# Batch 0's attention in two-bank tiles, scores in another order, and batch 1's loads moved off ScalarE: one attention + MLP kernel on one Trainium2 core

## The chip, the cores and the metric

The kernel runs on one NeuronCore of a Trainium2 chip. The metric is the device time of one execution in microseconds (us); before the change the median of five runs is 300.94 us (300.72 to 301.49). The engines are named as in the profile: PE is TensorE (PEld its weight loads), DVE VectorE, ACT ScalarE, POOL GpSimd, SP SyncE. ACTq and SPq are the instruction queues of ACT and SP when they issue a DMA.

## The reference

The computation is attention with pooled keys and values, followed by an MLP over all tokens. There are 8 batches, 8 heads, 576 tokens a batch and a head size of 64.

```python
k_p = k.reshape(B, H, Sp, 8, D).mean(axis=3)          # 576 keys become 72
v_p = v.reshape(B, H, Sp, 8, D).mean(axis=3)
scores = scale * np.matmul(q, k_p.transpose(0, 1, 3, 2))
scores = scores - np.max(scores, axis=-1, keepdims=True)
attn = np.exp(scores)
attn = attn / (np.sum(attn, axis=-1, keepdims=True) + 1e-09)
attn_out = np.matmul(attn, v_p)                       # [8, 8, 576, 64]
x = attn_out.transpose(0, 2, 1, 3).reshape(4608, 512)
h = x @ w_in                                          # [4608, 2048]
out = (h - np.tanh(h)) @ w_out                        # [4608, 512]
```

## The kernel before

**Attention of one batch.** Two heads have 144 pooled keys together, and the kernel calls this a pair. The first 128 key rows of each of the four pairs are one tile each; the 16 left over of each pair share a fifth tile, the leftover tile (index `NM`), at 32 rows a pair. `pool_k` adds the eight raw rows of each key, `turn_tile` transposes the pooled keys on PE, and `kb_main` and `kb_left` place them in `KB`. The queries are cast to bf16 (`q_turn` for batch 0, `q_cast` for the others) and transposed on PE (`q_pe_transpose`, one pair of heads a call). `scores_wide` multiplies them for 512 of the 576 query columns and ACT takes the exponential into `E`; the last 64 columns come later through `q_pe_tail` and `scores_tail`, which are called the tail. `av_half` multiplies `E` by the pooled values `VB` for one block of 128 queries and one half of the heads: three matmuls, the third for the leftover keys. `VB` carries a column of constants, so the sum of the exponentials comes out beside each head. DVE then takes the reciprocal of the four sums (L359) and multiplies (L360). The result `x_sb` is transposed into `xT`, for batches 0 and 1 on PE with a copy by ACT (`x_pe_transpose`, L390 and L397).

**MLP.** Tokens are worked in nine groups of 512. For each group there are 16 hidden blocks of four matmuls (L428, one for each feature block of `xT`), ACT's tanh (L439) and DVE's subtraction (L441); then four blocks of output tokens with 16 matmuls each (L456). Group 0 needs batch 0's attention alone. Batch 1's attention is woven into group 0's output matmuls, four of them at a step u = 0 to 15, and later batches into the group before the one that needs them.

**Order.** The order of the work on each engine is written out by hand: the program runs in the order of the source (`manual_schedule`), each engine takes its instructions in that order, and semaphores are set where one engine needs another's result. A DMA that is issued by an engine stands in that engine's order, with its waits.

**The head.** Nothing dense can run until batch 0's queries, keys and values are loaded, pooled, scored and normalised, and `xT` is filled. `warm_pe` puts matmuls with no use of their own into that time (L527). Batch 0's q comes in three loads that ACT issues (L534), its leftovers of k and v in two more (L111), its q tail in another (L640, between the second and third exponential). Its v is loaded as bf16 by POOL and pooled by PE (`v_pe_pool`, L618). The opening halves of hidden blocks 0 to 4 (`mlp_h_mms(0, i, 0, 2)`) are run as soon as feature blocks 0 and 1 of `xT` are there.

**Loads.** SP issues k, q and v of batch 1 after batch 0's k. The load of k waits for the second chunk of `w1` (L592). POOL issues the four chunks of `w1` (L503) and of `w2` (L510): two of `w2` early, and two inside `pool_k` of batch 1, after its first addition. The leftover of batch 1's v is four loads of 16 rows, and its q tail one load; ACT issues these five (L106, L127) behind batch 0's exponentials.

**PSUM.** Three pools share the eight banks: `ps_h` with three, `ps_o` with two and `ps_a` with three. `ps_any` takes from `ps_a` and `ps_h` in turn, and from `ps_a` alone once the opening halves run.

Of the kernel before, what the change touches and what calls it, by code (L numbers as in the profile page):

```python
# [8 lines left out]
FP32 = mybir.dt.float32  # L9
BF16 = mybir.dt.bfloat16  # L10
# [9 lines left out]
R = 4  # L20
# [5 lines left out]
TG = 512  # L26
# [11 lines left out]
def kernel(  # L38
# [19 lines left out]
    ps_h = ctx.enter_context(tc.tile_pool(name="ps_h", bufs=3, space=PSUM))  # L58
    ps_o = ctx.enter_context(tc.tile_pool(name="ps_o", bufs=2, space=PSUM))
    ps_a = ctx.enter_context(tc.tile_pool(name="ps_a", bufs=3, space=PSUM))  # L60
# [14 lines left out]
    spread = const.tile([128, 128], BF16, name="spread")  # L75
    mask = const.tile([128, 3 * NM, 1], FP32, name="mask")
# [3 lines left out]
    q_bf = const.tile([128, R + 1, H, D], BF16, name="q_bf")  # L80
    warm = const.tile([128, 1], FP32, name="warm")
# [22 lines left out]
    def load_left(src, dst, b, eng=nc.sync):  # L104
        return [
            eng.dma_start(out=dst[32 * t : 32 * t + LO, NM, :], in_=src[b, 128:PR, t, :])  # L106
            for t in range(NM)
        ]
# [35 lines left out]
    def q_cast(b, eng=nc.gpsimd.tensor_copy, parts=1):  # L144
        t = q_raws.pop(b)
        n = H // parts
        for h in range(0, H, n):
            eng(  # L148
                out=q_bf[:, 0:R, h : h + n, :].rearrange("p j h d -> p h j d"),
                in_=t[:, h : h + n, 0:R, :],  # L150
            )
        eng(out=q_bf[:QT, R, :, :], in_=t[:QT, :, R, :])
# [61 lines left out]
    def pool_v(b, eng):  # L214
        r = v_raw[b % 2].rearrange("p t (j d) -> p t j d", d=D)
        eng.tensor_tensor(  # L216
            out=r[:, :, 0:4, :], in0=r[:, :, 0:4, :], in1=r[:, :, 4:8, :], op=ALU.add
        )
        eng.tensor_tensor(  # L219
            out=r[:, :, 0:2, :], in0=r[:, :, 0:2, :], in1=r[:, :, 2:4, :], op=ALU.add  # L220
        )
        eng.tensor_tensor(
            out=r[:, :, 0, :], in0=r[:, :, 0, :], in1=r[:, :, 1, :], op=ALU.add
        )
        v_main(VB[b % 2], r[:, :, 0:1, :], eng, 0, NM)
        v_left(VB[b % 2], r[:, NM, 0:1, :], eng)

    def v_main(vb, vs, eng, t0, t1):
        n = t1 - t0
        eng.tensor_tensor(  # L230
            out=vb[:, 2 * t0 : 2 * t1, 0:D].rearrange("p (t s) d -> p t s d", s=2),
            in0=vs[:, t0:t1, :, :].to_broadcast([128, n, 2, D]),
            in1=mask[:, 2 * t0 : 2 * t1, :]
            .rearrange("p (t s) o -> p t s o", s=2)
            .to_broadcast([128, n, 2, D]),
            op=ALU.mult,
        )

# [82 lines left out]
    def scores_wide(b, ts):  # L321
        if b not in E_tiles:
            E_tiles[b] = work.tile([128, NT, S], BF16, name="E", tag="E")
        E = E_tiles[b]
        for t in ts:
            ps = ps_any([128, QA], FP32, "s_ps")
            score_mms(b, t, ps[:, :], 0, QA)
            nc.scalar.activation(out=E[:, t, 0:QA], in_=ps[:, :], func=ACT.Exp, scale=SCALE)

# [8 lines left out]
    def av_half(b, blk, half, x_sb, alloc):  # L338
        E = E_tiles[b]
        vb = VB[b % 2]  # L340
        c0 = blk * 128 if blk < 4 else S - 128
        ps = alloc([128, 4, D1], FP32, "x_ps")
        for n in range(3):
# [14 lines left out]
        rden = work.tile([128, 4, 1], FP32, name="rden", tag="rden", bufs=4)  # L358
        nc.vector.reciprocal(out=rden[:, :, :], in_=ps[:, :, D:D1])  # L359
        nc.vector.tensor_tensor(  # L360
            out=x_sb[:, half, :, :],
            in0=ps[:, :, 0:D],
            in1=rden[:, :, :].to_broadcast([128, 4, D]),
            op=ALU.mult,
        )
# [56 lines left out]
    def mlp_h_mms(g, i, f0, f1, pool=None):  # L422
        tok0 = g * TG
        if f0 == 0:
            p, tag = pool or (ps_h, "hT_ps")
            h_tiles[i] = p.tile([128, TG], FP32, name="hT_ps", tag=tag)
        for fb in range(f0, f1):
            nc.tensor.matmul(  # L428
                h_tiles[i][:, :],
                lhsT=w1b[:, fb, i * 128 : (i + 1) * 128],  # L430
                rhs=xT[:, fb, tok0 : tok0 + TG],
                start=(fb == 0),
                stop=(fb == NFB - 1),
            )
# [88 lines left out]
    warm_ps = ps_o.tile([128, 512], FP32, name="warm_ps", tag="o_ps")  # L523
# [60 lines left out]
    load_w2(0)  # L584
    nc.gpsimd.tensor_copy(out=v_bf[:, NM, :], in_=v_raw[1][:, NM, :])
    load_w2(1)
# [5 lines left out]
    after(load_k(1), w1_dmas[1])  # L592
    load_q(1, False)
    load_main(v_pairs, v_raw[1], 1, 0, NM)

# [19 lines left out]
    def v_pe_pool(t0, t1, turn):  # L615
        ps = ps_any([128, t1 - t0, 1, D], FP32, "v_ps")
# [26 lines left out]
    pool_k(0, nc.vector, 2, 4)  # L643
    warm_pe(6)
    k_turn(2, 4)
    pool_k(0, nc.vector, NM, NT)
    warm_pe(2)
    q_pe_transpose(0, (2, 3), "act")
    warm_pe(2)
    scores_wide(0, (2, 3))  # L650
    k_turn_left()
    warm_pe(2)
    v_ps = v_pe_pool(NM, NT, spread)
    scores_wide(0, (NM,))
    v_left(VB[0], v_ps[:, 0, :, :], nc.vector)
    vs = v_pe_pool(0, NM, ident)
    v_main(VB[0], vs, nc.vector, 0, 2)
    v_main(VB[0], vs, nc.vector, 2, 4)
    load_left(v_pairs, v_raw[1], 1, nc.scalar)
    load_q_tail(1, q_raws[1], nc.scalar)  # L660
    xs = [new_x() for _ in range(4)]
    gts = []
    ps_o2 = lambda sh, dt, name: ps_o.tile(sh, dt, name=name, tag="o_ps")
    ps_h2 = lambda sh, dt, name: ps_h.tile(sh, dt, name=name, tag="hT_ps")
    warm_pe(2)
    av_half(0, 0, 0, xs[0], ps_all)
    av_half(0, 1, 0, xs[1], ps_all)
    av_half(0, 2, 0, xs[2], ps_all)
    x_pe_transpose(0, 0, xs[0], (0, 2))
    av_half(0, 3, 0, xs[3], ps_all)  # L670
    warm_pe(1)
    x_pe_transpose(0, 1, xs[1], (0, 2))
    ps_any = ps_b1
    av_half(0, 0, 1, xs[0], ps_h2)
    warm_pe(1)
    x_pe_transpose(0, 2, xs[2], (0, 2))
    av_half(0, 1, 1, xs[1], ps_b1)
    warm_pe(1)
    x_pe_transpose(0, 3, xs[3], (0, 2))
    av_half(0, 2, 1, xs[2], ps_o2)  # L680
    mlp_h_mms(0, 0, 0, 2)
    x_pe_transpose(0, 0, xs[0], (2, 4))
    av_half(0, 3, 1, xs[3], ps_b1)
    mlp_h_mms(0, 1, 0, 2)
    x_pe_transpose(0, 1, xs[1], (2, 4))
    mlp_h_mms(0, 2, 0, 2)
    x_pe_transpose(0, 2, xs[2], (2, 4))
    x_pe_transpose(0, 3, xs[3], (2, 4))
    mlp_h_mms(0, 3, 0, 2, (ps_o, "o_ps"))
    mlp_h_mms(0, 4, 0, 2, (ps_o, "o_ps"))  # L690
# [16 lines left out]
    pool_k(1, nc.gpsimd, mid=(2, 3))  # L707
# [5 lines left out]
    for u in range(16):  # L713
        qd, tb = u // 4, u % 4
        mlp_o(0, tb, qd * 4, qd * 4 + 4, gts, o_pools[tb])
        if u == 0:
            q_cast(1, nc.scalar.copy, 2)
# [4 lines left out]
        if u == 4:  # L722
            q_pe_transpose(1, (2,), "act")
            pool_v(1, nc.vector)
        if u == 5:
            q_pe_transpose(1, (3,), "act")
        if 4 <= u <= 8:
            scores_wide(1, (u - 4,))
        if u == 6:
            q_pe_tail(1)  # L730
        if u == 8:
            scores_tail(1)
# [72 lines left out]
```

The softmax here doesn't subtract the row's maximum and nothing guards it: scores larger than these inputs give would overflow.

## Time and profile before

| what | us |
|---|---|
| median of five runs | 300.94 |
| the profiled execution, its own time | 300.52 |
| its span in the profile | 298.8 |
| PE busy | 289.7 (97%) |
| DVE busy | 159.1 (53%) |
| ACT busy | 149.3 (50%) |
| POOL busy | 115.5 (39%) |
| first AV matmul of batch 0 starts | 14.51 |
| first opening half of a hidden block starts | 18.68 |

A row in order of time gives the start, the length, the engine, the line, the operation and what it writes and reads; in brackets stands how long the engine was idle before it and what ended that. Matmuls follow one another faster than one takes: the 512-column ones are listed with 379 ns each and start every 0.216 us when nothing holds them. Some matmul records are missing from the trace. A wait for several semaphores is put down to the one that the profile saw last.

### The profile page before, as it was taken

How to read it: one execution, taken by the hardware profiler on the slowest of the kernel's cores; microseconds unless marked ns; L12 is line 12 of the kernel's file. 1: busy time of each engine (PE TensorE's matmuls, PEld its weight loads, DVE VectorE, ACT ScalarE, POOL GpSimd, SP SyncE). 2: the span in 40 equal slices, each digit the busy share in tenths (PEclk: the TensorE clock that was granted, in tenths of full speed). 3: DMA queues.
4: the chain of work that ended last, by engine and by line, in shares of the span. 5: the costliest groups of instructions: out<-in, count | busy, mean ns of one | idle time of the engine just before them, and what ended most of it. 6: DMA issues, size and time to landing. Idle time of an engine off the chain costs nothing.

```text
span 298.8 us, 4663 instructions
## 1 busy us (share of the span) xinstructions
PE 289.7 (97%) x1640; PEld 142.8 (48%) x1671; DVE 159.1 (53%) x343; ACT 149.3 (50%) x283; POOL 115.5 (39%) x110
## 2 busy tenths in 40 slices
PE   7989999999999999999999999999999999999994
PEld 3444456444544454445544554455445544444443
DVE  5658666683547444753476247715680758008600
ACT  4747683666246623654266416651666066126511
POOL 8500903971396109921991099207940000000000
PEclk9999999999999999999999999999999999999999
DMA  7999999859955997499648964897431430111032
GB/s 256 223 211 280 308 228 328 241 89 322 243 112 105 270 296 129 95 284 289 106 87 235 313 155 93 253 304 138 97 66 35 91 97 0 37 70 36 2 70 70
DMA packets 66183, 49.79 MB, mean 167 GB/s; under 512 B 39920, under 2 KB 52976, under 8 KB 66160
## 3 DMA queue, kind: packets, MB, share of 16 engines
q1 hardware_dynamic: 58832, 42.94, 55.4%
q0 software_dynamic: 4752, 4.72, 9.4%
q10 hardware_dynamic: 2576, 1.84, 2.2%
q8 instruction: 13, 0.21, 0.3%
q14 instruction: 10, 0.08, 0.1%
HBM read 36.70 MB, written 9.44 MB: 154 GB/s over the span
## 4 chain that ended last, share of the span: by engine, by line
PE 84%; DMA 9%; POOL 4%; issue 1%; SPq 0%; ACT 0%; DVE 0%; POOLq 0%
PE o_ps L456 39%; PE hT_ps L428 37%; DMA w1b<-in_moe_w_in_dram 4%; PE x_ps L346 4%; DMA k_raw<-in_k_dram 4%; PE s_ps L298 3%; POOL k_raw L198 1%; DMA out_dram<-o_sb 1%; POOL k_raw L203 1%; POOL kd L206 1%; POOL w2b L510 0%; PE xT_ps L390 0%; POOL v_raw L576 0%; PE qT_ps L171 0%; POOL w1b L503 0%
## 5 line engine op out<-in xcount | busy, mean ns | idle before, releaser
L456 PE MATMUL o_ps<-w2b,gT 128*128 128x512 bf16 x542 | 131.8, 379 | 0.9 <-issue 0.2
L441 DVE TENSOR_TENSOR gT<-hT_ps,t_sb 128x512 bf16<-128x512 f32 x144 | 98.9, 691 | 57.4 <-ACT t_sb L439 57.3
L428 PE MATMUL hT_ps<-xT,w1b 128*128 128x512 bf16 x564 | 126.1, 379 | 0.9 <-ACT xT L397 0.3
L439 ACT ACTIVATE t_sb<-hT_ps 128x512 f32<-128x512 f32 x144 | 85.6, 597 | 38.3 <-PE hT_ps L428 37.5
L428 PEld LDWEIGHTS <-w1b 128*128 128x128 bf16 x576 | 56.0, 98 | 66.4 <-issue 0.4
L456 PEld LDWEIGHTS <-gT 128*128 128x128 bf16 x560 | 52.6, 98 | 52.0 <-issue 1.4
L465 ACT COPY o_sb<-o_ps 128x512 f32<-128x512 f32 x33 | 19.3, 585 | 75.2 <-PE o_ps L456 72.3
L359 DVE RECIPROCAL rden<-x_ps 128x4 f32<-128x4 f32 x80 | 14.1, 176 | 52.6 <-PE x_ps L346 52.1
L360 DVE TENSOR_TENSOR x_sb<-x_ps,rden 128x256 bf16<-128x256 f32 x80 | 33.9, 424 | 3.9 <-DMA xT<-x_sb 0.9
L148 POOL CAST q_bf<-q_raw 128x2048 bf16<-128x2048 f32 x6 | 11.3, 1888 | 60.1 <-issue 35.3
L198 POOL TENSOR_TENSOR k_raw<-k_raw 128x1280 f32<-128x1280 f32 x7 | 20.2, 2886 | 28.2 <-DMA k_raw<-in_k_dram 28.2
L317 ACT ACTIVATE E<-s_ps 128x288 bf16<-128x288 f32 x60 | 21.4, 410 | 13.2 <-PE s_ps L298 13.0
L346 PE MATMUL x_ps<-VB,E 128*128 128x130 bf16 x240 | 20.8, 220 | 0.7 <-ACT xT L397 0.6
L346 PEld LDWEIGHTS <-E 128*128 128x128 bf16 x240 | 16.9, 98 | 9.1 <-issue 0.7
L216 POOL TENSOR_TENSOR v_raw<-v_raw 128x1280 f32<-128x1280 f32 x6 | 17.4, 2898 | 0.0
L298 PE MATMUL s_ps<-qT,KB 128*128 128x288 bf16 (+5 forms) x128 | 17.0, 289 | 0.3
L298 PEld LDWEIGHTS <-KB 128*128 128x128 bf16 (+1 forms) x128 | 7.0, 96 | 10.1 <-issue 3.5
L527 PE MATMUL warm_ps<-xT 128*128 128x512 bf16 x28 | 10.0, 469 | 1.3 <-DVE xT L539 1.3
L206 POOL TENSOR_TENSOR kd<-k_raw 128x640 bf16<-128x640 f32 x7 | 10.8, 1540 | 0.5
L203 POOL TENSOR_TENSOR k_raw<-k_raw 128x640 f32<-128x640 f32 x7 | 10.8, 1543 | 0.5
L397 ACT CAST xT<-xT_ps 128x256 bf16<-128x256 f32 (+1 forms) x14 | 5.8, 436 | 8.8 <-PE xT_ps L390 8.6
L219 POOL TENSOR_TENSOR v_raw<-v_raw 128x640 f32<-128x640 f32 x6 | 9.2, 1541 | 0.5
(73 smaller groups left out, 100.9 us busy)
## 6 DMA issues: line engine op xcount, KB each, us to landing
k_raw<-in_k_dram SPq DMA_DIRECT2D x7, 1024.0 KB, 6.6
q_raw<-in_q_dram SPq DMA_DIRECT2D x7, 1024.0 KB, 9.5
v_raw<-in_v_dram SPq DMA_DIRECT2D x7, 1024.0 KB, 9.1
out_dram<-o_sb SPq DMA_DIRECT2D x38, 128.0 KB, 2.5
out_dram<-o_sb SPq DMA_DIRECT2D x16, 256.0 KB, 3.5
w1b<-in_moe_w_in_dram POOLq DMA_DIRECT2D x4, 512.0 KB, 13.9
w2b<-in_moe_w_out_dram POOLq DMA_DIRECT2D x4, 512.0 KB, 17.0
k_raw<-in_k_dram SPq DMA_DIRECT2D x7, 128.0 KB, 6.6
```

The lines of the kernel that those rows point to most:

```text
L198: first = eng.tensor_tensor(out=r[:, :, 0:4, :], in0=r[:, :, 0:4, :], in1=r[:, :, 4:8, :], op=ALU.add)
L216: eng.tensor_tensor(out=r[:, :, 0:4, :], in0=r[:, :, 0:4, :], in1=r[:, :, 4:8, :], op=ALU.add)
L298: nc.tensor.matmul(dst[p : p + w], lhsT=KB[b % 2][:, o : o + w], rhs=qTs[b][:, m, c0:c1], start=True, stop=True,)
L317: nc.scalar.activation(out=E[:, t, half * hs : (half + 1) * hs], in_=ps[:, :], func=ACT.Exp, scale=SCALE)
L346: nc.tensor.matmul(ps[:, 2 * n : 2 * n + 2, :].rearrange("p h d -> p (h d)") if n < 2 else ps.rearrange("p (a s) d -> p a s d", s=2)[:, :, ...
L359: nc.vector.reciprocal(out=rden[:, :, :], in_=ps[:, :, D:D1])
L360: nc.vector.tensor_tensor(out=x_sb[:, half, :, :], in0=ps[:, :, 0:D], in1=rden[:, :, :].to_broadcast([128, 4, D]), op=ALU.mult,)
L428: nc.tensor.matmul(h_tiles[i][:, :], lhsT=w1b[:, fb, i * 128 : (i + 1) * 128], rhs=xT[:, fb, tok0 : tok0 + TG], start=(fb == 0), stop=(fb ...
L439: nc.scalar.activation(out=t_sb[:, :], in_=h_ps[:, :], func=ACT.Tanh)
L441: nc.vector.tensor_sub(out=gT[:, :], in0=h_ps[:, :], in1=t_sb[:, :])
L456: nc.tensor.matmul(o_ps[:, :], lhsT=gts[i][:, tb * 128 : (tb + 1) * 128], rhs=w2b[:, i, :], start=(i == 0), stop=(i == NHID - 1),)
L465: (nc.vector.tensor_copy if g == 0 and tb % 2 else nc.scalar.copy)(out=o_sb[:, :], in_=o_ps[:, :])
```

## The change

PSUM becomes one tile of eight banks that are named by number; `Banks` gives the old three pools' turns. What moves:

- **Loads.** The leftover of batch 1's v is one dense load on SP, ahead of q; batch 1's q tail goes to SP behind v. Batch 1's k waits for the first chunk of `w1` alone, its leftover for none. POOL runs `pool_k` of batch 1 before the head's code instead of after group 0's hidden blocks, with the first chunk of `w2` ahead of it (after the third chunk of `w1`), the second inside it and two behind it.
- **Batch 0's scores.** The leftover keys' pooling by DVE moves ahead of pair 2's and 3's placement; the leftover scores come ahead of those of pairs 2 and 3. `VB` of pairs 2 and 3 is made by ACT (`v_main_act`), that of pairs 0 and 1 by DVE.
- **Batch 0's AV.** `av_pair` puts two blocks of queries into two neighbouring banks and normalises both with one reciprocal (128x8) and one multiply (128x512). `x0_turn` transposes two blocks at once.
- **Batch 1.** The dense leftover is pooled by DVE (`pool_v1`), spread by one matmul (`v1_left`) at u = 8. The q tail's cast moves to u = 5, its transposes from u = 6 to 9, the tail scores from u = 8 to 11.

```diff
+    ps_h = Banks(0, 1, 2)
+    ps_o = Banks(3, 4)
+    ps_a = Banks(5, 6, 7)
...
+    def pool_v1(eng):
+        r = v_raw[1].rearrange("p t (j d) -> p t j d", d=D)
...
+        eng.tensor_tensor(
+            out=vl[:, :], in0=r[:, NM, 0, :], in1=r[:, NM, 1, :], op=ALU.add
+        )
...
+    def v1_left():
+        ps = ps_any([128, 1, D], FP32, "v_ps")
+        nc.tensor.matmul(ps[:, 0, :], lhsT=spread[:, :], rhs=vl[:, :], start=True, stop=True)
+        v_left(VB[1], ps, nc.vector)
...
+    def v_main_act(vb, vs, t0, t1):
+        for h in range(2):
+            nc.scalar.activation(
+                out=vb[:, 2 * t0 + h : 2 * t1 : 2, 0:D],
+                in_=vs[:, :, 0, :],
+                func=ACT.Copy,
+                scale=mask[:, h, :],
+            )
...
-    load_w2(0)
     nc.gpsimd.tensor_copy(out=v_bf[:, NM, :], in_=v_raw[1][:, NM, :])
-    load_w2(1)
...
-    after(load_k(1), w1_dmas[1])
+    k1 = load_k(1)
+    after(k1[:1], w1_dmas[0])
+    load_dense(v_pairs, v_raw[1], 1)
     load_q(1, False)
     load_main(v_pairs, v_raw[1], 1, 0, NM)
+    load_q_tail(1, q_raws[1], nc.sync)
+    load_w2(0)
+    after(w2_dmas, w1_dmas[2])
+    pool_k(1, nc.gpsimd, mid=(1,))
+    load_w2(2)
+    load_w2(3)
...
     pool_k(0, nc.vector, 2, 4)
+    pool_k(0, nc.vector, NM, NT)
     warm_pe(6)
     k_turn(2, 4)
-    pool_k(0, nc.vector, NM, NT)
+    q_pe_transpose(0, (2,), "act")
+    warm_pe(1)
+    q_pe_transpose(0, (3,), "act")
+    k_turn_left()
+    warm_pe(3)
+    v_ps = v_pe_pool(NM, NT, spread)
+    v_left(VB[0], v_ps[:, 0, :, :], nc.vector)
+    scores_wide(0, (NM, 2, 3), (2, 5, 6))
+    v_a = v_pe_pool(0, 2, ident, 3)
+    v_main(VB[0], v_a, nc.vector, 0, 2)
+    v_b = v_pe_pool(2, 4, ident, 7)
+    v_main_act(VB[0], v_b, 2, 4)
+    gts = []
+
+    def av_pair(p, half, b0):
+        ps = PS[:, b0 : b0 + 2, 0 : 4 * D1].rearrange("p k (h d) -> p k h d", d=D1)
+        for k in range(2):
+            av_mms(0, 2 * p + k, half, ps[:, k, :, :])
+        rden = work.tile([128, 2, 4, 1], FP32, name="rden2", tag="rden2")
+        nc.vector.reciprocal(out=rden[:, :, :, :], in_=ps[:, :, :, D:D1])
+        nc.vector.tensor_tensor(
+            out=x0[:, 2 * p : 2 * p + 2, half, :, :],
+            in0=ps[:, :, :, 0:D],
+            in1=rden[:, :, :, :].to_broadcast([128, 2, 4, D]),
+            op=ALU.mult,
+        )
...
+    av_pair(0, 0, 0)
+    av_pair(1, 0, 2)
+    av_pair(0, 1, 5)
     warm_pe(2)
-    q_pe_transpose(0, (2, 3), "act")
+    x0_turn((0, 1), 0, 7, nc.scalar.copy)
+    av_pair(1, 1, 0)
     warm_pe(2)
-    scores_wide(0, (2, 3))
-    k_turn_left()
+    x0_turn((2, 3), 0, 2, nc.scalar.copy)
     warm_pe(2)
-    v_ps = v_pe_pool(NM, NT, spread)
-    scores_wide(0, (NM,))
-    v_left(VB[0], v_ps[:, 0, :, :], nc.vector)
-    vs = v_pe_pool(0, NM, ident)
-    v_main(VB[0], vs, nc.vector, 0, 2)
-    v_main(VB[0], vs, nc.vector, 2, 4)
-    load_left(v_pairs, v_raw[1], 1, nc.scalar)
-    load_q_tail(1, q_raws[1], nc.scalar)
...
+    x0_turn((0, 1), 1, 7, nc.scalar.copy)
+    h_open(3, 3)
+    h_open(4, 4)
+    x0_turn((2,), 1, 5, nc.scalar.copy)
+    x0_turn((3,), 1, 6, nc.vector.tensor_copy)
+    h_open(2, 2)
+    h_open(0, 0)
+    h_open(1, 1)
...
-    pool_k(1, nc.gpsimd, mid=(2, 3))
...
         if u == 0:
-            q_cast(1, nc.scalar.copy, 2)
+            q_cast(1, nc.scalar.copy, 2, False)
...
         if u == 4:
             q_pe_transpose(1, (2,), "act")
-            pool_v(1, nc.vector)
+            pool_v1(nc.vector)
         if u == 5:
             q_pe_transpose(1, (3,), "act")
+            q_cast_tail(1, nc.scalar.copy)
...
-        if u == 6:
+        if u == 8:
+            v1_left()
+        if u == 9:
             q_pe_tail(1)
-        if u == 8:
+        if u == 11:
             scores_tail(1)
```

`h_open(i, b0)` runs the opening half of hidden block i in bank b0; `x0_turn` holds four transposing matmuls for two blocks, or two for one, and one copy. The load of batch 0's q tail stays where it was in ACT's order, between the second exponential and the casts of heads 4 to 7.

## The prediction

> **What bounds the kernel now.** I read the page first, then the matrix engine's gaps, then the first 22 us in order of time, then the landings of the loads.
>
> ```profile
> PE 289.7 (97%) x1640; PEld 142.8 (48%) x1671; DVE 159.1 (53%) x343; ACT 149.3 (50%) x283; POOL 115.5 (39%) x110
> PE 84%; DMA 9%; POOL 4%; issue 1%; SPq 0%; ACT 0%; DVE 0%; POOLq 0%
> ```
>
> The first line is the busy time of each engine, the second the chain that ended last. TensorE (PE) is busy for 97% of the span, so the change can only win or lose where PE waits. Those places are few: behind 21 us the list of waits names hardly any. They lie in the head, before batch 0's MLP runs densely. The head in order of time (start, length, engine, line, what):
>
> ```profile
> 8.25 0.65 ACTq L640 DMA_DIRECT2D q_raw<-in_q_dram  x1
> 8.99 1.14 ACT L610 CAST q_bf<-q_raw 128x512 bf16<-128x512 f32 x2
> 9.97 0.61 PE L171 MATMUL qT_ps<-ident,q_bf 128*128 128x128 bf16 x8
> 10.54 0.72 POOL L585 CAST v_raw<-v_raw 128x512 bf16<-128x512 f32 x1 [1.72 <-DMA v_raw<-in_v_dram]
> 13.13 1.76 ACTq L106 DMA_DIRECT2D v_raw<-in_v_dram  x4
> 14.03 0.76 DVE L230 TENSOR_TENSOR VB<-v_ps,mask 128x256 bf16<-128x256 f32 x2 [0.81 <-PE v_ps L618]
> 14.51 0.69 PE L346 MATMUL x_ps<-VB,E 128*128 128x130 bf16 x9
> 14.90 0.18 DVE L359 RECIPROCAL rden<-x_ps 128x4 f32<-128x4 f32 x1
> 15.12 0.42 DVE L360 TENSOR_TENSOR x_sb<-x_ps,rden 128x256 bf16<-128x256 f32 x1
> 16.46 0.62 ACTq L127 DMA_DIRECT2D q_raw<-in_q_dram  x1
> 17.13 0.92 ACT L397 CAST xT<-xT_ps 128x256 bf16<-128x256 f32 x3 [3.47 <-PE xT_ps L390]
> 17.55 0.34 PE L346 MATMUL x_ps<-VB,E 128*128 128x130 bf16 x3 [0.57 <-ACT xT L397]
> 18.68 0.59 PE L428 MATMUL hT_ps<-xT,w1b 128*128 128x512 bf16 x2 [0.29 <-ACT xT L397]
> 20.80 5.56 PE L428 MATMUL hT_ps<-xT,w1b 128*128 128x512 bf16 x25
> ```
>
> See ACT: it casts nothing from 13.66 to 17.13, and starts 0.04 us after its last load (L127) is issued, though the first transpose (15.60, 0.28 long) was ready before 16. L127 itself starts at 16.46, because batch 0's q tail (issued 8.25, 8.2 us to landing) landed at 16.44 and both use one completion semaphore. A load that waits on an engine's queue holds up all compute behind it. PE then waits on ACT's casts (0.57 and 0.29). Second, the chain behind the head (start, length, what):
>
> ```profile
> 5.85 12.55 DMA w1b<-in_moe_w_in_dram
> 18.89 10.88 DMA k_raw<-in_k_dram
> 29.94 2.89 POOL k_raw L198
> 32.83 1.47 POOL w2b L510 x2
> 35.96 1.55 POOL kd L206
> 37.55 0.45 PE kT_ps L259 x5
> ```
>
> Batch 1's k waits for the second w1 chunk (18.40), and its pooling ends at 37.51, when PE is just there: the last o matmul before it starts at 37.10 and needs 0.216, so PE loses 0.24. And the landings of three loads (KB each, us from issue):
>
> ```profile
> v_raw<-in_v_dram ACTq DMA_DIRECT2D x1, 128.0 KB, 7.3
> w1b<-in_moe_w_in_dram POOLq DMA_DIRECT2D x1, 512.0 KB, 10.1
> w1b<-in_moe_w_in_dram POOLq DMA_DIRECT2D x1, 512.0 KB, 12.5
> ```
>
> Batch 0's dense v leftover, issued at 3.07, lands at 10.4 (POOL's cast at 10.54 agrees); w1's chunks land at 15.2 and 18.4.
>
> **The change part by part.** I compare one point: the first matmul of feature blocks 2 and 3 of hidden block 0, from which the PE work is the same. Before: the 25 listed from 20.80 are 26 (one record is missing; 26 weight loads stand beside them, and the next group starts at 26.20), so they began at 26.20 − 26 × 0.2156 = 20.60; four belong to the opening half, so the point is 20.60 + 0.86 = 21.46.
>
> *Loads off ACT.* Five issues (1.76 + 0.62 us) and their waits go, and with them the hole to 17.13. They go to SP's queue: the dense v leftover, which waits for POOL's cast of the rows that it overwrites (done at 11.26), stands ahead of batch 1's q and v, the q tail behind them. But the completion semaphores are handed out in turn, and in the built program the slots move: batch 0's q tail, still issued by ACT behind the first two exponentials, now takes the slot of the dense v leftover and waits for it. It had no such wait. So instead of 8.25 it is issued at 10.42, and behind it in ACT's order stand the two q casts of heads 4 to 7 (L610): 10.42 + 0.65 + 0.04 = 11.11 instead of 8.99. That is 2.12 us late on the path, and pairs 2 and 3 wait for it: PE has nothing from 9.65 (pair 2's k turn) to 11.77.
>
> *The new head from 11.11*, each step by its row. Casts end 11.72 and 12.25 (pitch 0.53). PE turns q pair 3 at 12.30, copies on ACT 12.27 to 13.35. PE in order: k leftover 12.52, three warm-up matmuls (0.216 each) to 13.23, v leftover pooling (0.32), leftover scores (0.33), scores 2 and 3 (0.43), eight pooling matmuls of pairs 0 and 1 (first at 14.31, last at 14.71). VB on DVE 0.27 after that, 0.42 long: 15.39; first AV 0.06 later at 15.45 (before: 14.51). ACT meanwhile: exponentials 14.0 to 15.6 (pitch 0.49), then the two scaled copies of VB 4 to 7, bounded by the 0.20 of a 128x1 and the 0.37 of a 128x256 row: done by 16.1, ahead of their use. Six AV matmuls (pitch 0.057) and 0.27: first reciprocal at 16.0.
>
> *One normalisation per pair.* Before, one half costs DVE 0.22 (start to start of reciprocal and multiply) + 0.34: eight halves 4.5 us. A multiply of 512 columns is not in this line; the gT subtraction, 128x512 from PSUM, takes 691 ns, the 256-column one 424, so I take 0.69 and a pair costs 0.22 + 0.61 = 0.83, four 3.3. Bounds: twice 0.42 (no gain) and 0.69. The multiplies end at 16.9, 17.75, 18.6 and 19.4, against 20.23 for the last one before: the late start is won back.
>
> *Turns and opening halves.* Turn (0,1) at 16.98, the last AV pair 0.22 later, two warm-ups to 17.97, turn (2,3) 17.97; its ACT copy starts 18.40 and takes 0.58 (the 128x512 row 0.589): 18.98. Opening halves from 19.04: ten matmuls 2.16, four more turn matmuls 0.22, three gaps of about 0.02: the point is at 21.47. **Head: 0.0 us.** Bounds: −0.8 (below, rival A) and +0.8 (each of some fifteen handovers 0.05 worse than its row).
>
> *DMA order.* k of batch 1 now waits for w1's first chunk (15.2, not 18.4). Before, the chunk in flight when k was released landed 3.5 later (21.9), so the second now lands near 18.75; its first user, opening half 4, comes at 19.47. w1's third and fourth near 23.3 and 28.2 (4.6 and 4.8 each before), wanted at 26.5 and 30.6. POOL issues w2's first chunk only after the third w1 chunk; near 32.8, wanted at 34.5 (landed 31.3 before). k lands at 15.25 + 10.8 = 26.1, its leftover 0.6 later, pooled by 33.5 with a w2 issue between, wanted at 37.1. That w2 chunk lands near 37.1, wanted at 39.2; the last two are issued about as before (33.5), wanted at 44 and 48. So the 0.24 goes: **−0.24** (bounds −0.24 and 0). On SP's queue q follows near 34, v 38 to 40.5, q's tail 0.5 to 1 later; DVE wants v by 42.6, and what queues behind the tail's cast on ACT is four exponentials, whose first use is the bank of scores 4 at 45: nothing.
>
> *Tail scores moved to u = 11.* With three banks in turn, the second AV half of block 2 now writes the bank that the tail's exponential still reads. Tail matmuls 0.36, turn 0.22, first half 0.17: ready after 0.75; the exponential ends 0.46 + 0.43 + 0.06 = 0.95 after the first tail matmul. Before, four o matmuls (0.86) stood between. **+0.2 to +0.3**, I take 0.25 (bounds 0 and 0.43, the whole exponential). The extra leftover matmul and its gap: **+0.05**. The banks named by hand make DVE and ACT wait for each other's earlier reads of a bank; all of those end before PE rewrites it, so nothing.
>
> *The rule that I weigh.* The granted clock's row is 9 tenths in all slices, so only the pitch tells: nine warm-ups take 4.02 us from 1.26 (0.43 each), six take 1.46 from 8.05 (0.216). No row shows what a 2.1 us hole does, so nothing is charged; charged at the cold pitch, it is rival B and 303.0. The Trainium skill (TensorE: Matmul & The Clock Gate, Part 1 and the table row on throughput drops) says the array returns to half rate only after a whole idle window of about 3.4 us; by that the hole is free, and the sum stays as it is.
>
> **Sum.** 0.0 − 0.24 + 0.25 + 0.05 = +0.06 on the profiled execution's 300.52 (span 298.8), which lies 0.42 under the median of the five runs, 300.94. So **301.0 us**.
>
> **The rivals.** *A, faster.* The q tail's wait costs nothing, since the leftover lands early or the engine passes the load by. For it: only one trace's 10.4 stands behind the wait. Against: L127 shows just such a hold. Even then opening half 4 waits for w1's second chunk near 18.75, so the point is not before 18.75 + 0.43 + 0.22 + 1.29 = 20.7: −0.76, giving 300.2.
> *B, slower.* PE falls to the half rate in or after its hole. From 12.3 to 14.8 PE works without a pause; these 2.4 us double but for some 0.4 of the small matmuls' gaps: +2.0, 303.0. It decides if the pitch of the three warm-ups near 12.6 is 0.43. For it: the hole is the longest after the start. Against: holes of 0.8 in before left 0.216.
> *C, slower.* k's transfer, released 3.2 us earlier, slows the second w1 chunk: at the contended 4.6 it lands at 19.8, +0.35 on opening half 4, and handovers add 0.4: 301.8. It decides beyond 19.5.
>
> **How the numbers follow.** Forecast 0.45, A 0.20, B 0.08, C 0.27. About 0.2% (0.6 us) is what a measurement here can tell from no change. The forecast spreads 300.4 to 301.5. Faster takes A; same the forecast and a little of C; slower the rest of C and B: 0.20, 0.48, 0.32. The range reaches A's time and C's, and leaves out B and what goes beyond A: 300.1 to 302.3.
>
> **What would show it.** ACT's load at 10.4 with the casts at 11.1; AV near 15.4; four reciprocal and multiply pairs of 0.83; dense PE from 19.0; the k turn of batch 1 without a wait; a wait of 0.2 to 0.3 before an AV matmul near 50. I am wrong if the q tail is issued near 8.3, if the chunks of w1 or w2 hold PE, or if matmuls in the head show 0.43.

## The result, and the profile after

The changed kernel takes 301.87 us in the median of 32 runs (300.45 to 304.0), the kernel before 300.90 in 55 (300.24 to 301.96). The ratio is 1.0027 with a 95% interval of 1.0017 to 1.0036: slower by 0.27%. The forecast of 301.0 said no change to be measured; 301.87 lies inside its range of 300.1 to 302.3, 0.87 above the forecast.

The profiled execution shows none of this. It takes 300.56 us (span 298.9, mean granted TensorE clock 0.998), 0.04 more than the profiled execution before. The runs fall apart by their granted clock:

```
mean granted clock     executions   us
0.997 to 1.0           10           300.45 to 300.73, and one of 301.72
0.992 to 0.994         20           301.72 to 302.81
0.988                   2           303.85, 304.0
```

The median of the first ten is 300.6, of the twenty 302.0. So the profile is of the smaller group, and it has to be read as what the change does while the clock stays whole. From the page, the busy time and the chain that ended last (by engine):

```profile
PE 289.1 (97%) x1647; PEld 143.3 (48%) x1679; DVE 158.2 (53%) x336; ACT 149.2 (50%) x281; POOL 115.4 (39%) x110
PE 93%; DMA 3%; DVE 1%; issue 1%; ACT 0%; ACTq 0%; DVEq 0%
```

The chain runs elsewhere now. Before, 9% of it was DMA and 4% POOL (w1, batch 1's k, its pooling); now the only load in it is this one, in order of time (start, us):

```profile
3.05 7.47 DMA v_raw<-in_v_dram
```

That is the dense v leftover of batch 0, landing at 10.52. The head after it, in order of time (start, length, engine, line, what; in brackets the idle time before and what ended it):

```profile
9.91 0.28 PE L317 MATMUL PS<-ident,kd 128*128 128x128 bf16 x2 [0.26 <-DVE kd L234]
10.55 0.65 ACTq L707 DMA_DIRECT2D q_raw<-in_q_dram  x1
11.24 1.14 ACT L676 CAST q_bf<-q_raw 128x512 bf16<-128x512 f32 x2 [2.12 <-DMA v_raw<-in_v_dram]
11.91 0.40 PE L199 MATMUL PS<-ident,q_bf 128*128 128x128 bf16 x4 [1.72 <-ACT q_bf L676]
12.72 0.81 PE L587 MATMUL PS<-xT 128*128 128x512 bf16 x3
18.75 0.20 DVE L733 RECIPROCAL rden<-PS 128x8 f32<-128x8 f32 x1
18.98 0.69 DVE L734 TENSOR_TENSOR x<-PS,rden 128x512 bf16<-128x512 f32 x1
19.28 1.02 PE L488 MATMUL PS<-xT,w1b 128*128 128x512 bf16 x4
20.36 6.21 PE L488 MATMUL PS<-xT,w1b 128*128 128x512 bf16 x28
```

The q tail's load goes out 0.02 us after the leftover has landed, the casts follow, and TensorE has a hole of 1.72. The three warm-up matmuls behind it take 0.81: in this execution the clock is whole. Of the matmuls from 20.36, six still belong to opening halves, so the point that the prediction compares comes at 20.36 + 6 × 0.2156 = 21.65. Later in the same view, batch 1's attention:

```profile
37.53 0.44 PE L317 MATMUL PS<-ident,kd 128*128 128x128 bf16 x5
...
39.15 1.03 PE L516 MATMUL PS<-w2b,gT 128*128 128x512 bf16 x4
49.23 0.71 PE L415 MATMUL PS<-VB,E 128*128 128x130 bf16 x6
```

The k turn no longer waits. The six AV matmuls at 49.23 take 0.71 where such a group takes 0.51 elsewhere: they wait 0.20 for the tail's exponential. The matmuls at 39.15 are the first that need the second w2 chunk; it landed at 38.98.

### The profile page after: what moved, and what is told of

The parts are those of the page before. It is cut to its first block, busy times and chain, and to the rows that moved or that the text cites. A ratio compares the mean times of both kernels' runs of the same rounds, so it can differ in the third digit from the quotient of the medians.

```text
span 298.9 us, 4689 instructions
## 1 busy us (share of the span) xinstructions
PE 289.1 (97%) x1647; PEld 143.3 (48%) x1679; DVE 158.2 (53%) x336; ACT 149.2 (50%) x281; POOL 115.4 (39%) x110
## 4 chain that ended last, share of the span: by engine, by line
PE 93%; DMA 3%; DVE 1%; issue 1%; ACT 0%; ACTq 0%; DVEq 0%
PE PS L488 41%; PE PS L516 40%; PE PS L415 5%; PE PS L356 4%; DMA v_raw<-in_v_dram 3%; PE PS L537 1%; PE PS L587 1%; PE PS L199 1%; PE PS L451 0%; PE PS L746 0%; DVE x_sb L401 0%; PE PS L685 0%; DVE gT L501 0%; ACTq L707 0%; ACT q_bf L676 0%
## 5 line engine op out<-in xcount | busy, mean ns | idle before, releaser
L516 PE MATMUL PS<-w2b,gT 128*128 128x512 bf16 x542 | 132.0, 379 | 0.9 <-issue 0.2
L501 DVE TENSOR_TENSOR gT<-PS,t_sb 128x512 bf16<-128x512 f32 x144 | 98.9, 691 | 57.5 <-ACT t_sb L499 57.3
L488 PE MATMUL PS<-xT,w1b 128*128 128x512 bf16 x564 | 126.0, 379 | 0.6
L499 ACT ACTIVATE t_sb<-PS 128x512 f32<-128x512 f32 x144 | 85.6, 597 | 38.9 <-PE PS L488 37.9
L525 ACT COPY o_sb<-PS 128x512 f32<-128x512 f32 x33 | 19.3, 586 | 75.3 <-PE PS L516 75.3
L400 DVE RECIPROCAL rden<-PS 128x4 f32<-128x4 f32 x72 | 12.7, 177 | 51.0 <-PE PS L415 50.7
L401 DVE TENSOR_TENSOR x_sb<-PS,rden 128x256 bf16<-128x256 f32 x72 | 30.5, 424 | 2.8 <-DMA xT<-x_sb 0.3
L375 ACT ACTIVATE E<-PS 128x288 bf16<-128x288 f32 x60 | 21.4, 409 | 13.2 <-PE PS L356 13.0
L415 PE MATMUL PS<-VB,E 128*128 128x130 bf16 x240 | 20.3, 220 | 0.1
L356 PE MATMUL PS<-qT,KB 128*128 128x288 bf16 (+5 forms) x127 | 16.7, 289 | 0.4 <-issue 0.2
```

Source lines behind the costliest of these rows:

```text
L356: nc.tensor.matmul(dst[p : p + w], lhsT=KB[b % 2][:, o : o + w], rhs=qTs[b][:, m, c0:c1], start=True, stop=True,)
L375: nc.scalar.activation(out=E[:, t, half * hs : (half + 1) * hs], in_=ps[:, :], func=ACT.Exp, scale=SCALE)
L401: nc.vector.tensor_tensor(out=x_sb[:, half, :, :], in0=ps[:, :, 0:D], in1=rden[:, :, :].to_broadcast([128, 4, D]), op=ALU.mult,)
L415: nc.tensor.matmul(ps[:, 2 * n : 2 * n + 2, :].rearrange("p h d -> p (h d)") if n < 2 else ps.rearrange("p (a s) d -> p a s d", s=2)[:, :, ...
L488: nc.tensor.matmul(h_tiles[i][:, :], lhsT=w1b[:, fb, i * 128 : (i + 1) * 128], rhs=xT[:, fb, tok0 : tok0 + TG], start=(fb == 0), stop=(fb ...
L499: nc.scalar.activation(out=t_sb[:, :], in_=h_ps[:, :], func=ACT.Tanh)
```

## The experiments

The theory after the result (**theory 1**): TensorE's hole ahead of the late casts lets its clock fall for a while in most executions. **Theory 2**: the two groups come from the new order of the loads. **Theory 3**: the late casts cost the time themselves. Each kernel is compared with runs of the kernel before on the same chip: medians 300.83, 300.85 and 300.55 in the three sets (experiments 1 to 4, 5 to 8, 9 to 12). "Dip" stands for an execution with a mean granted clock of 0.995 or less; of the 99 runs of the kernel before in these sets, one has it.

**1. The hole filled.**

```diff
     k_turn(2, 4)
+    warm_pe(8)
     q_pe_transpose(0, (2,), "act")
```

> The changed kernel with eight more 512-column warm-up matmuls between the k turn of pairs 2 and 3 and the q transposes of pair 2, that is inside TensorE's hole from 9.98 to 11.91. The q tail's load still waits on ACT and the casts are still 2.1 us late. Theory 1 (the hole lets TensorE's clock fall in about two of three executions, and that is the 1.3 us between the two groups of the changed kernel's times): no slow group, the granted clock 0.998 to 1.0 in all executions, median 300.5 to 300.7. Theory 2 (the two groups come from the new order of the loads, which the fill does not touch): two groups as before, 300.5 and 301.9, median near 301.9. Theory 3 (the late casts cost the time by themselves): median 301.9 without two groups.

No dip in 12 executions (clock 0.998 to 1.0); median 301.16 (300.39 to 301.99), ratio 1.0005 (0.9994 to 1.0017). In order of time:

```profile
11.03 1.14 ACT L676 CAST q_bf<-q_raw 128x512 bf16<-128x512 f32 x2 [2.23 <-DMA v_raw<-in_v_dram]
11.70 0.40 PE L199 MATMUL PS<-ident,q_bf 128*128 128x128 bf16 x4 [0.36 <-ACT q_bf L676]
20.14 2.10 PE L488 MATMUL PS<-xT,w1b 128*128 128x512 bf16 x9
```

The casts are as late as before, the loads as they were, and the dips are gone: theory 1 holds against both rivals for the dips. But the median came out 0.5 over what I expected, and the times spread over 1.6 us with the clock whole. Something else moves them; experiments 5 to 9 look for it.

**2. The wait taken away.** The lines that load batch 1 are written behind `q_turn(nc.scalar.copy, 6, 8)`; each engine's order stays, but the q tail's load takes another completion semaphore.

```diff
-    k1 = load_k(1)
     ...
     nc.scalar.dma_start(out=t0[:QT, :, R, :], ...)
     q_turn(nc.scalar.copy, 4, 6)
     q_turn(nc.scalar.copy, 6, 8)
+    k1 = load_k(1)
     ...
```

> The changed kernel with the loads of batch 1 written behind batch 0's q tail in the source. No engine's order changes; only the completion semaphores are handed out in another turn, so that the q tail's load takes the one of the first q load and no longer waits for the dense v leftover. Expected of theory 1: load issued near 8.3 instead of 10.55, casts of heads 4 to 7 from 9.0, no hole of TensorE over 0.8 us, the granted clock 0.998 to 1.0 in every execution; the opening halves from about 17.2 instead of 19.28, and the second of them held by the second w1 chunk near 18.2, so the head is won by about 1.5 us: 299.0 to 299.5. Theory 2: the head is won as well, but the two groups stay, 299.0 and 300.4. Theory 3: as theory 1 in the median, since the late casts are gone too.

Median 300.65 (300.25 to 301.14), ratio 0.9993 (0.9984 to 1.0002), one dip in 11. In order of time:

```profile
8.22 0.65 ACTq L694 DMA_DIRECT2D q_raw<-in_q_dram  x1
9.22 1.14 ACT L663 CAST q_bf<-q_raw 128x512 bf16<-128x512 f32 x2 [0.33 <-DMA q_raw<-in_q_dram]
18.87 6.21 PE L488 MATMUL PS<-xT,w1b 128*128 128x512 bf16 x28
...
39.12 1.02 PE L516 MATMUL PS<-w2b,gT 128*128 128x512 bf16 x4 [1.30 <-DMA w2b<-in_moe_w_out_dram]
```

The head is won as expected: dense at 18.87 instead of 20.36, 1.49 earlier. Most of it is given back at one place: TensorE comes to the second w2 chunk 1.5 earlier and waits 1.30 for it. The chain that ended last has loads in it again, 10%, w1, k and w2 in turn. I had expected 299.0 to 299.5 and had not looked at what is late next.

**3. A hole in the kernel before.**

```diff
     pool_k(0, nc.vector, 2, 4)
-    warm_pe(6)
     k_turn(2, 4)
```

> The kernel before without the six warm-up matmuls ahead of the k turn of pairs 2 and 3. They have no use of their own, and nothing waits for them, so the schedule stays; TensorE has only the k turn's two matmuls between about 8.0 and 9.97. Theory 1: a hole is enough by itself, so a part of the executions shows a granted clock of 0.994 or less and a time 1.3 us longer; if the threshold lies above 2.0 us, none does and the median stays 300.9. Theories 2 and 3: 300.9, no second group, since neither loads nor casts are changed.

No dip in 11; median 300.85, ratio 1.0001 (0.9992 to 1.001). The hole came out shorter than expected: 1.30 in the list of waits (1.5 with the other wait for the same tile, `kd`). A hole of this size isn't enough.

**4. The hole of the changed kernel made longer**, by leaving out the same six warm-up matmuls.

> The changed kernel without the same six warm-up matmuls: TensorE has next to nothing from about 8.2 to 11.91, 3.7 us instead of 1.9 (2.6 with the gap before the k turn). Theory 1: all executions in the slow group or worse, clock 0.992 or less, median 302 to 303. Theories 2 and 3: no change against the changed kernel, median near 301.9 with the share of its two groups as it was.

All 8 executions dip; median 302.31 (301.48 to 303.36), ratio 1.0047 (1.0031 to 1.0064). Four have 0.994 and 301.5 to 302.0, four 0.987 to 0.992 and 302.6 to 303.4. Its profile fell into a dip, and so did that of experiment 7. Stretches of both traces (the window; busy time and count of PE, PEld, DVE, ACT and POOL; then the granted clock, DMA share, GB/s), first the one of this kernel:

```profile
7.70:11.11 3.41, 0.62 (x3) 0.11 (x2) 2.96 (x8) 1.18 (x3) 1.08 (x3) 1.00 1.16 238
11.11:14.52 3.41, 2.86 (x17) 1.76 (x18) 0.38 (x2) 2.19 (x4) 1.50 (x3) 0.50 1.24 204
```

The clock is 0.50 for 3.41 us, from 11.11 to 14.52, and whole on both sides (edges from half-microsecond windows). One such dip in a span of 300 gives a mean of 1 − 1.705/300 = 0.994. Two would give 0.989, near the lowest group's 0.988, but no trace holds two. No trace of the changed kernel itself holds a dip either; experiment 7, which differs from it only in when one load is issued, has one.

**5 and 6. The second w2 chunk issued earlier**, on the kernel of experiment 1 and on that of experiment 2.

```diff
-    pool_k(1, nc.gpsimd, mid=(1,))
+    load_w2(1)
+    pool_k(1, nc.gpsimd)
```

> The kernel with the filled hole, and POOL issues the second w2 chunk right behind the first, ahead of the pooling of batch 1's k, instead of inside it (at 29.5 in the filled kernel). Theory 4: with the clock whole, what spreads the filled kernel's times from 300.4 to 302.0 is that chunk, which landed 38.8 in its profile, 0.3 ahead of its first user at about 39.1; in the slow ones it comes later than its user. Then the times close up: all within 300.2 to 300.8, median 300.4 to 300.6, the chunk landing near 36 to 37. If theory 4 is wrong, the median stays near 301.2 and the spread 1.5 us wide.

> The kernel without the q tail's wait, with the same earlier issue of the second w2 chunk. Without it TensorE waited 1.30 us for this chunk at 39.12, which is what the head had won. Theory 4: the wait is gone or below 0.3, and the median falls by 1.0 to 1.3 us, to 299.3 to 299.7. If the next chunk or batch 1's q or k takes its place, it stays at 300 to 300.6 with another wait between 36 and 46 us.

Both miss. With the fill: median 301.07 (300.55 to 301.73), ratio 1.0003 (0.9993 to 1.0013). Without the wait: 300.85 (300.25 to 301.86), ratio 0.9991 (0.9976 to 1.0005). In the latter the chunk is issued in the pair at 23.12 instead of at 29.50, and TensorE still gets it at 39.13 (in order of time):

```profile
23.12 1.50 POOL L570 DMA_DIRECT2D w2b<-in_moe_w_out_dram  x2 [10.19 <-DMA w1b<-in_moe_w_in_dram]
39.13 1.02 PE L516 MATMUL PS<-w2b,gT 128*128 128x512 bf16 x4 [0.83 <-DMA w2b<-in_moe_w_out_dram]
```

The profile of experiment 5 (301.33 us) shows something that moves the time and has nothing to do with w2. Its v leftover landed later; the q tail was issued at 10.97, the casts began at 11.67 and the dense matmuls at 20.79. From casts to dense that is 9.12; in the changed kernel's profile it is 20.36 − 11.24 = 9.12 and in experiment 1's 9.11. In these three traces the head follows one landing, microsecond for microsecond, because of the wait.

**7. The same edit on the changed kernel**, hole and wait left in.

> The changed kernel with its hole and its q tail's wait, and only the earlier second w2 chunk. Theory 1 (clock): the two groups stay, one of 300.3 to 300.6 with the clock at 0.997 to 1.0 and one of 301.6 to 302.2 with 0.992 to 0.994, the second in about two of three executions, median 301.8. If the late chunk and not the clock made the slow group: one group, 300.4 to 300.6.

Ten dips in 12; median 302.12 (300.88 to 303.09), ratio 1.0035 (1.002 to 1.0051); the two executions without a dip are the two fastest. The w2 chunk doesn't make the groups. The trace, with a dip, by stretches and in order of time:

```profile
8.90:12.31 3.41, 0.45 (x3) 0.11 (x2) 3.02 (x8) 0.56 (x2) 1.14 (x3) 1.00 1.19 203
12.31:15.72 3.41, 3.30 (x25) 2.11 (x25) 0.47 (x2) 1.75 (x4) 0.97 (x2) 0.50 1.23 204
```

```profile
11.74 1.14 ACT L677 CAST q_bf<-q_raw 128x512 bf16<-128x512 f32 x2 [3.26 <-DMA v_raw<-in_v_dram]
12.42 0.61 PE L199 MATMUL PS<-ident,q_bf 128*128 128x128 bf16 x4 [1.83 <-ACT q_bf L677]
13.78 1.49 PE L587 MATMUL PS<-xT 128*128 128x512 bf16 x3
22.31 1.03 PE L488 MATMUL PS<-xT,w1b 128*128 128x512 bf16 x4
```

Again 3.41 us at 0.50. The three warm-up matmuls take 1.49, a pitch of 0.43: the mark that the prediction named for rival B. From casts to dense it is 10.57 instead of 9.12: the dip costs 1.45 here, and in experiment 4 (10.99 to 21.40, 10.41) 1.30.

**8. The tail two steps earlier**, on the kernel of experiment 6.

```diff
-        if u == 9:
+        if u == 7:
             q_pe_tail(1)
-        if u == 11:
+        if u == 9:
             scores_tail(1)
```

> The kernel without the q tail's wait and with the earlier second w2 chunk, and with batch 1's tail two steps earlier, the q tail's transposes at u = 7 and the tail scores at u = 9. My step on the tail: the wait of 0.20 on the tail's exponential near 49.5 goes, so 0.2 us less than the same kernel with the tail at 9 and 11. If the wait only moves to another reader of the bank, the two are equal.

Median 301.74 (300.74 to 303.28), ratio 1.0023 (1.0007 to 1.0038), three dips in 12. The wait of 0.20 is gone and a longer one stands in its place (in order of time):

```profile
43.96 0.62 ACT L169 CAST q_bf<-q_raw 64x512 bf16<-64x512 f32 x1 [1.84 <-DMA q_raw<-in_q_dram]
45.12 0.28 PE L211 MATMUL PS<-ident,q_bf 128*128 128x64 bf16 x4 [1.25 <-ACT E L386]
```

Batch 1's q tail, on SP behind v, lands at 43.94 here, and ACT's cast of it holds the exponentials behind it. The move of the tail to u = 9 and 11 and the load's move to SP belong together; the 0.20 is the smaller price.

**9. v held back**, on the kernel of experiment 6.

```diff
-    load_main(v_pairs, v_raw[1], 1, 0, NM)
+    after([load_main(v_pairs, v_raw[1], 1, 0, NM)], w1_dmas[3])
```

> The kernel without the q tail's wait and with the second w2 chunk issued early, and batch 1's main v load held until the fourth w1 chunk has landed (27.9). Theory 5: the second w2 chunk lands at 38.7 to 39.1 however early it is issued, since the bytes ahead of it in the queues set it; with v's 1 MB out of its way it lands near 36.5, TensorE's wait of 0.8 to 1.3 us at 39.1 goes, and the median falls to 299.6 to 300.2. If v or the third w2 chunk takes its place (they are wanted at 40 to 42.6), the gain is below 0.3 and a wait stands between 39 and 46. If the chunk still lands at 39, theory 5 is wrong.

Theory 5 is wrong in the part that I could act on: v goes out at 28.00 instead of 18.6, the chunk lands at 38.92 all the same, and TensorE waits (in order of time):

```profile
38.96 1.02 PE L516 MATMUL PS<-w2b,gT 128*128 128x512 bf16 x4 [1.29 <-DMA w2b<-in_moe_w_out_dram]
```

Median 300.86, ratio 1.0008 (1.0 to 1.0017). What the loads have in common is seen in one stretch of the kernel before, the changed one and this one (columns as above, the last two DMA share and GB/s):

```profile
15.00:39.00 24.00, 22.25 (x148) 11.24 (x148) 16.89 (x40) 15.58 (x30) 7.47 (x5) 1.00 1.17 266
```

```profile
15.00:39.00 24.00, 23.45 (x166) 12.51 (x167) 16.80 (x34) 15.70 (x29) 8.94 (x7) 1.00 1.16 266
```

```profile
15.00:39.00 24.00, 22.39 (x147) 11.16 (x145) 15.96 (x32) 15.59 (x27) 8.95 (x7) 1.00 1.16 264
```

In all three orders the DMA engines are busy all through (share 1.16 to 1.17) and move 264 to 266 GB/s on average, some 6.4 MB in these 24 us. Only the shares change: the kernel before has its second w2 chunk at 35.65 and k at 29.21, the changed one has k at 26.01 and the chunk at 38.98. Why the chunk didn't come sooner with v held back isn't settled; v's landing at 40.46 says that it still ran beside it.

**10. Normalisation by halves**, on the kernel of experiment 1: in `av_pair`, two reciprocals of 128x4 and two multiplies of 128x256 for a pair.

```diff
-        nc.vector.reciprocal(out=rden[:, :, :, :], in_=ps[:, :, :, D:D1])
+        for k in range(2):
+            nc.vector.reciprocal(out=rden[:, :, :], in_=ps[:, k, :, D:D1])
...
```

> The kernel with the filled hole, and batch 0's AV normalised by halves again (two reciprocals of 128x4 and two multiplies of 128x256 for each pair) in the same two-bank tiles. My step says a half takes 0.56 of DVE and a pair 0.83, so DVE's four pairs take 4.5 us instead of 3.35. From the start of the casts of heads 4 to 7 to the dense matmuls the filled kernel takes 9.11 us. If DVE sets the head there, this becomes 10.0 to 10.3 and the median rises by up to 1.1; if ACT's turns or PE's order set it, it stays below 9.4.

Median 300.98, ratio 1.0019 (1.001 to 1.0028), no dip. In order of time:

```profile
11.03 1.14 ACT L676 CAST q_bf<-q_raw 128x512 bf16<-128x512 f32 x2 [2.22 <-DMA v_raw<-in_v_dram]
15.83 0.18 DVE L735 RECIPROCAL rden<-PS 128x4 f32<-128x4 f32 x1 [0.49 <-ACT VB L290]
19.89 0.42 DVE L736 TENSOR_TENSOR x<-PS,rden 128x256 bf16<-128x256 f32 x1
20.49 0.81 PE L488 MATMUL PS<-xT,w1b 128*128 128x512 bf16 x3
```

From casts to dense 9.46, 0.35 more, which is between my two cases. DVE's chain is 1.0 longer (15.83 to 20.31, where experiment 1 has 16.00 to 19.45), but it starts 0.17 earlier, since one block is enough to begin, and experiment 1 had 0.47 to spare between the last multiply and its turn on TensorE at 19.92. So the two-bank normalisation is worth 0.35 us of the head and not 1.1. The median shows no loss beside experiment 11's in the same set.

**11. The hole half filled** (`warm_pe(4)` instead of 8).

> The kernel with the hole half filled, four warm-up matmuls instead of eight, which leaves TensorE idle for about 1.4 us before the q transposes. Theory 1: a hole of 1.4 us makes few or no slow executions (none of 11 in the kernel before with a hole of 1.46), one of 1.9 makes two of three: at most 2 of 12 with a clock of 0.994 or less, and the median 301.0 to 301.2, as with eight. If the clock falls at random in whatever hole, half of the executions show it.

No dip in 11; median 301.06 (300.44 to 301.31), ratio 1.0011 (1.0002 to 1.0019). The hole is 1.1 in the list of waits, where 1.4 was expected. Its head is that of experiment 1 (casts 11.03), but its w2 chunk landed at 39.59, and its profiled execution is 0.7 longer (in order of time):

```profile
39.63 1.02 PE L516 MATMUL PS<-w2b,gT 128*128 128x512 bf16 x4 [0.53 <-DMA w2b<-in_moe_w_out_dram]
```

So the filled kernels have two loads without slack, the v leftover in the head and the second w2 chunk. That their times spread by these two is read from three single traces (300.39, 301.07 and 301.33 us); no run tests it.

**12. One part alone, on the kernel before**: no loads on ACT.

```diff
-    load_main(v_pairs, v_raw[1], 1, 0, NM)
...
-    load_left(v_pairs, v_raw[1], 1, nc.scalar)
-    load_q_tail(1, q_raws[1], nc.scalar)
+    load_q_tail(1, q_raws[1], nc.sync)
+    load_left(v_pairs, v_raw[1], 1)
+    load_main(v_pairs, v_raw[1], 1, 0, NM)
```

> The kernel before with one part of the change alone: batch 1's q tail, the four v leftover loads and the main v load go to SP behind q, and ACT issues none of them. ACT then casts the first transpose at about 15.9 instead of 17.13, and TensorE's waits of 0.57 and 0.29 in the head go, so the head is won by 0.5 to 0.8 us. By the chain of batch 1's k, which ends at 37.5 whatever the head does, TensorE then waits 0.7 to 1.0 us for it instead of 0.24, and the median stays at 300.7 to 301.0. If the head is worth something by itself, the median is 300.2 to 300.5.

Median 300.55, ratio 1.0005 (0.9995 to 1.0016): no change, as expected, but not quite where I expected it. In order of time:

```profile
15.82 0.37 ACT L397 CAST xT<-xT_ps 128x256 bf16<-128x256 f32 x1 [2.26 <-PE xT_ps L390]
19.88 1.46 PE L428 MATMUL hT_ps<-xT,w1b 128*128 128x512 bf16 x6
36.62 0.44 PE L259 MATMUL kT_ps<-ident,kd 128*128 128x128 bf16 x5
39.70 0.38 PE L298 MATMUL s_ps<-qT,KB 128*128 128x512 bf16 x1 [0.20 <-ACT qT L96]
46.32 0.72 PE L346 MATMUL x_ps<-VB,E 128*128 128x130 bf16 x6
```

ACT casts at 15.82 instead of 17.13, and the dense matmuls begin at 19.88 instead of 20.60: 0.72 won in the head. Here w1's second chunk and k came earlier too (17.95 and 28.29), so the k turn doesn't wait. The gain goes at 39.70 (0.20) and around 46.3 (0.30 ahead of the AV matmuls, which start after `VB`, and 0.21 within them: 0.72 instead of 0.51), since v now lands at 42.57. The times stand in two groups, six of 300.12 to 300.55 and five of 300.98 to 301.43, all with the clock whole; that isn't explained.

No version beats the kernel before by more than its interval; experiments 2 and 6 come nearest.

## Why the prediction was right and wrong

**Right, with the clock whole.** The q tail's wait was forecast for 10.42 and came at 10.55, the casts at 11.11 and 11.24, TensorE's hole to 11.77 and 11.91. The first AV matmul was put at 15.45 and came at 15.60, the pair of reciprocal and multiply at 0.83 and took 0.84, the last multiply ends at 19.67 instead of 19.4. The point of comparison is at 21.65, not 21.47: the head term was +0.19 instead of 0.0, of which 0.13 is the load that landed later in this execution. Batch 1's k wait went (−0.24 as said), the tail cost 0.20 (0.25 said). The sum of +0.06 us met +0.04 between the two profiled executions. That is closer than its terms: with the extra leftover matmul (0.04), the terms as measured make +0.19, and where the other 0.15 went isn't traced.

**Inside the range by luck.** The median came 0.87 above the forecast. It lies inside the range because the upper end was set for rival C, which did not come. The range was said to leave out rival B, and it is B's mechanism that came, at a lower price.

**The step that failed** is the one headed "The rule that I weigh": "No row shows what a 2.1 us hole does, so nothing is charged". With a hole of 1.72 to 1.83 in the traces, the mean granted clock fell to 0.994 or less in 22 of 32 executions of the changed kernel and in 10 of 12 of experiment 7, whose trace shows it as 3.41 us at half rate; where the hole is filled, it fell in none. As more than half of the executions dip, the median takes the whole price: the ten without a dip have 300.6, and 1.3 more is 301.9. Rival B had the mechanism and its mark, but a chance of 0.08. What was set against it is misread: in the trace before, the longest hole of TensorE after the start is 0.57 and not 0.8. Its price of 2.0 was too high: measured were 1.30 and 1.45. In experiment 4 the first 0.55 of the dip falls into the end of the hole, in experiment 7 the first 0.11; that small matmuls with gaps lose less is the likely rest, not shown. I let a rule decide where a bound from both sides was due, and carried the 0.42 between one profiled execution and the median over to a kernel whose executions fall into two groups.

The Trainium skill (TensorE: Matmul & The Clock Gate, Part 1) has the length of its window right, 3413 ns against the measured 3.41 us, and it says that the window runs freely, which agrees with the same hole dipping in some executions only. Its condition of an idle window, which made the hole look free, the runs contradict: the 3.41 us ahead of the two dips held 0.45 and 0.62 us of TensorE work, and the longest stretch without any in them was 1.73 and 1.47.

**Rival A** said that without the wait the second w1 chunk would hold the head at 300.2. Experiment 2 is that case: the chunk landed at 18.16 and cost 0.16; what took the gain was the second w2 chunk. **Rival C** did not come: w1's second chunk landed at 18.19.

**A margin mis-sized.** "That w2 chunk lands near 37.1, wanted at 39.2": it landed at 38.98, wanted at 39.15. The margin was 0.2 instead of 2.1, without effect on the sum, but it is why winning the head gave nothing in experiment 2.

**What the loss is made of**, from ratios: filling the hole takes the kernel from 1.0027 to 1.0005 (0.9994 to 1.0017), taking the wait away to 0.9993 (0.9984 to 1.0002); neither can be told from no change.

## What to carry to other kernels

A wait that opens a hole of two microseconds in TensorE's work is to be charged with a clock dip times its chance, even where the profiled execution shows none; look at the granted clock of every execution, and fill the hole with matmuls that nothing waits for. Before counting a head's gain, find the next load whose landing time doesn't move with it: here the DMA engines are busy all through from 15 to 39 us, and of the 1.49 us that TensorE won in the head in experiment 2 it waited off 1.30 at 39.12. And when loads move between queues, look at which completion semaphore each later load inherits.

## What the runs showed of the hardware

This is how much TensorE worked in a stretch of 3.41 us in each profile, and how often the clock dipped. For experiments 4 and 7 the stretch is the one right ahead of the dip; where no dip was in the trace, it is the least busy one around its hole.

```
kernel                     PE busy of 3.41 us   dips
experiment 4               0.62                 8 of 8
experiment 7               0.45                 10 of 12
changed kernel             1.44                 22 of 32
hole half filled (11)      2.05                 0 of 11
kernel before, hole (3)    1.98                 0 of 11
two waits of 1.3 (8)       2.12                 3 of 12
wait of 1.3 at 39 (2)      2.11                 1 of 11
```

The changed kernel's row and then that of experiment 11, from the stretches of their traces:

```profile
8.50:11.91 3.41, 1.44 (x8) 0.42 (x6) 3.10 (x8) 1.29 (x4) 1.25 (x3) 1.00 1.19 202
```

```profile
8.29:11.70 3.41, 2.05 (x11) 0.62 (x9) 2.60 (x8) 1.00 (x3) 1.25 (x3) 1.00 1.21 214
```

Both traced dips came right behind a stretch with TensorE busy for 13% and 18%; the traces with 58% or more in their least busy stretch belong to kernels that seldom dip. Where between these the limit lies isn't shown by this table alone, since the changed kernel's 1.44 is from an execution that did not dip.

What that execution shows is where the stretches begin. At the start of a run matmuls go at half rate, and the moment when they speed up differs from trace to trace. In order of time, first from experiment 4, then from the changed kernel:

```profile
1.26 3.59 PE L587 MATMUL PS<-xT 128*128 128x512 bf16 x9 [1.26 <-DVE xT L599]
```

```profile
6.67 0.63 PE L199 MATMUL PS<-ident,q_bf 128*128 128x128 bf16 x4
7.10 0.68 PE L587 MATMUL PS<-xT 128*128 128x512 bf16 x2
```

In experiment 4 the nine warm-up matmuls take 3.59 instead of 4.02, so the clock rose near 4.3, and the dip begins at 11.11, two stretches of 3.41 later. In experiment 7 the k turn at 5.07 still goes at half rate (0.31) and the four transposes at 5.75 at the full one (0.40); two stretches ahead of its dip at 12.31 is 5.49. In the changed kernel's trace four transposes at 6.67 still take 0.63 (0.40 at the full rate), and from the two warm-ups behind them the rise works out near 7.27. Counted from there, the hole falls into two stretches:

```profile
7.27:10.68 3.41, 2.67 (x13) 0.89 (x10) 2.31 (x6) 1.67 (x3) 0.83 (x3) 1.00 1.15 255
10.68:14.09 3.41, 2.18 (x25) 1.31 (x27) 1.69 (x6) 2.21 (x4) 2.09 (x4) 1.00 1.24 205
```

Neither is as idle as the 1.44 of the table, and this execution did not dip. So where the hole lies in a freely running window can tell one execution of the same kernel from the next. An estimate from the single traces: laid at all places in turn, the window finds a stretch under 1.9 us of work in about seven places of ten in the changed kernel's trace, in all of them in those of experiments 4 and 7, and in none in the other four. The 1.9 is picked to meet the 22 of 32, so the other rows are its check; it leaves the three dips of experiment 8, the one of experiment 2 and the two executions of experiment 7 without a dip unexplained. That the busy share of such a window decides was argued from these traces and not tested by itself. A dip lasted 3.41 us in both traces that hold one, although TensorE worked almost all through it.
